# Decode block on one core: wq and wo in one load each, x in four one-row loads, the last PSUM copy on ScalarE

## Chip, core and metric

The kernel runs on one core of a Trainium2 chip. The metric is the device time of one execution in microseconds (us). A core has TensorE (PE, matmul; PEld is its weight load), VectorE (DVE), ScalarE (ACT), GpSimd (POOL) and the sync engine SP, which here issues nearly all loads. Sixteen DMA engines move the data from HBM into the on-chip memory SBUF. Matmuls write PSUM.

## What is computed

One token (x: 1024 numbers, bf16) passes an attention block with a cache and then a gated feed-forward block, each behind a layernorm and with a residual.

```python
q = layernorm(x) @ wq                       # wq 1024 x 4096: 32 heads of 128
k, v = repeat(k_cache, 8), repeat(v_cache, 8)   # 4 kv heads x 65536 positions x 128
p = softmax(q k^T * 128**-0.5)
h = x + (p v) @ wo                          # wo 4096 x 1024
out = h + (gelu(ln(h) @ w_gate) * (ln(h) @ w_up)) @ w_down   # 1024 x 3584 twice, 3584 x 1024
```

The two caches are 64 MB each, wq and wo 8 MB each, the three feed-forward weights 7 MB each: 173.02 MB are read once (counted in millions of bytes), and there is little arithmetic on each byte.

## The kernel before

**The ring.** All large operands go through one SBUF tile, `ring`, of five slots of 16384 bf16 a partition (`CW`, `NBUF`, lines 47 and 48). `load()` (lines 160 to 168) takes the next slots in turn by the counter `at[0]` and issues one load on SP's queue. SP works its issues off in order, and each one waits until the last reader of its slots is done. A K load (`kv_load`, lines 269 to 272) takes one slot, 32 KB to each of 128 partitions; a V load takes two slots, 64 KB to each.

**Start.** ScalarE issues x as one load of four rows of 256 (line 172), which land on partitions 0, 32, 64 and 96 of `x_row`. wq comes in two loads of 4 MB into slots 0 and 1 (lines 174 to 177); the first load is moved to the very front of SP's program (`first_load_leads`, lines 109 to 122). VectorE turns x into columns (line 219) and `layernorm_cols` (lines 197 to 216) makes `xn_bf`, which `padded` spreads out into `xnz`. Eight steps of eight matmuls (lines 246 and 247) make q in `q_ps`, four for each wq load. Copies to SBUF (`evac`, lines 235 to 239: even ones on VectorE, odd ones on ScalarE), transposes and casts then give `wsel` (line 262), the stationary operand of all K scores.

**Attention.** The hand-written list `todo` (lines 378 to 382) sets the order of the 24 K and V loads, and of the work on them. For a K tile VectorE turns four pieces in place (line 281), TensorE makes 32 score matmuls into `qk_ps` (lines 289 to 292), and ScalarE and VectorE copy the scores and take the maximum (lines 301 and 302). For half a V load (one slot) TensorE runs 32 matmuls (lines 340 to 344). The last three V loads are (2, 2), (3, 0) and (3, 2): kv head 2's second half, then kv head 3's two halves. By the counter they lie in slots 3 and 4, in 0 and 1, and in 2 and 3. `v_evac` and `v_end` close a head.

**After attention.** wo comes in two loads of 4 MB (lines 456 and 457), by the counter into slots 4 and 0. w_gate is one load of two slots (line 513; slots 1 and 2), w_up two loads of one slot (line 518; slots 3 and 4), and w_down five loads of falling size laid out one behind the other from slot 0 (lines 538 to 557, `at[0] = 0`). `row_mm` (lines 445 to 449) makes wo's 64 matmuls, c = 0 to 15 from the first load. The residual x is added on TensorE into `f_ps`, the second layernorm gives `hnz`, and gate and up follow. The down matmuls add into `f_ps` as well; `keep_busy` puts matmuls without a use between them. VectorE copies `f_ps` to `o_fin` (line 558), and SP stores it.

Of the kernel before, what the change touches and what calls it, by code (L numbers as in the profile page):

```python
# [17 lines left out]
def kernel(  # L18
# [13 lines left out]
    nc = tc.nc  # L32
    P = 128
    D = A_x.shape[-1]
    Hkv, Sk, Dh = A_k_cache.shape[1], A_k_cache.shape[2], A_k_cache.shape[3]
    HD = A_wq.shape[1]
    Hq = HD // Dh
    rep = Hq // Hkv
    F = B_w_gate.shape[1]
    DC = D // P  # L40
# [6 lines left out]
    CW = 16384  # L47
# [19 lines left out]
    x_row = lead.tile([P, D // 4], BF16, name="x_row")  # L67
# [12 lines left out]
    o_fin = const.tile([P, D // 4], BF16, name="o_fin")  # L80
# [61 lines left out]
    def mm(out, lhsT, rhs, start, stop, loaded=False, tile_position=None, skip_group_check=False):  # L142
        t = nc.tensor
        if not loaded:
            return pe(t.matmul(out, lhsT=lhsT, rhs=rhs, start=start, stop=stop, tile_position=tile_position,  # L145
                               skip_group_check=skip_group_check))
        op = t.add_instruction(mybir.InstMatmult(  # L147
            name=nc.get_next_instruction_name(), engine=t.engine, start_tensor_calc=start, stop_tensor_calc=stop,
            tile_size=(lhsT.shape[0], lhsT.shape[1]), tile_position=tile_position or (0, 0), ldweights=False,
            bass_skip_group_check=skip_group_check,  # L150
            ins=[t.lower_ap(rhs), t.lower_ap(lhsT, for_matmul_weights=True)], outs=[t.lower_ap(out, opt=True)]))
        reuses.add(op.ins.name)
        return pe(op)
# [4 lines left out]
    at = [0]  # L158

    def load(src, off=0):  # L160
        n, w = src.shape[1], src.shape[2]
        units = -(-(off + n * w) // CW)
        o = at[0] * CW + off
        assert o + n * w <= NBUF * CW
        at[0] = (at[0] + units) % NBUF
        tv = ring[:, o:o + n * w]
        nc.sync.dma_start(out=tv.rearrange("p (n w) -> p n w", w=w), in_=src)
        return tv.rearrange("p (n w) -> p n w", w=w)

    wq_v = A_wq.rearrange("(p c) n -> p c n", c=DC)  # L170
    nc.vector.memset(x_row[:], 0.0)
    nc.scalar.dma_start(out=x_row[0:97:32, :], in_=A_x[0, 0].rearrange("(g n) -> g n", g=4))
    assert DC * HD == 2 * CW and DC % 2 == 0
    wq_tiles = []
    for c0 in range(0, DC, DC // 2):
        wq_t = load(wq_v[:, c0:c0 + DC // 2, :])
        wq_tiles.extend(wq_t[:, i, :] for i in range(DC // 2))

    make_identity(nc, ident_bf[:])
    make_identity(nc, ident_f[:])  # L180
# [11 lines left out]
    for bp in range(4):  # L192
        s0 = 64 * (bp // 2) + bp % 2
        nc.vector.tensor_copy(out=esel[:, bp, :, :],
                              in_=ident_bf[:, s0:s0 + 63:2].unsqueeze(1).to_broadcast([P, 4, 32]))
# [27 lines left out]
    def padded(pool, vec, ncols, name, tag=None):  # L223
        t = pool.tile([P, ncols, 32], BF16, name=name, tag=tag or name)
        nc.gpsimd.memset(t[:], 0.0)
        nc.vector.tensor_copy(out=t[:, :, 0], in_=vec)
        return t
# [214 lines left out]
    def row_bank(name):  # L442
        return ps_w.tile([P, 512], F32, name=name, tag="w")

    def row_mm(banks, stat, w2, c, first, last):
        g = c % 4
        for s in range(DS):
            mm(banks[s][32 * g:32 * g + 32, :], stat, w2[:, s * 512:(s + 1) * 512], first, last,
               loaded=(s > 0), tile_position=(0, 32 * g))

    o2z = padded(rows, o2_ps[:], Hq, "o2z")
    wo_v = A_wo.rearrange("(p c) n -> p c n", p=P)
    WN = CW // D
    assert Hq % WN == 0
    at_ps = [row_bank("at_ps") for _ in range(DS)]
    for wc in range(Hq // WN):
        wv = load(wo_v[:, wc * WN:(wc + 1) * WN, :])
        for cc in range(WN):
            c = wc * WN + cc
            row_mm(at_ps, o2z[:, c, :], wv[:, cc, :], c, c < 4, c + 4 >= Hq)  # L460
    at_r = rows.tile([P, DS, 512], F32, name="at_r")
    for s in range(DS):
        evac(at_r[:, s, :], at_ps[s][:], s)
# [1 line left out]
    f_ps = ps_f.tile([P, OW], F32, name="f_ps")  # L465

    def out_mm(stat, mov, first, last, groups=range(4)):
        for g in groups:
            mm(f_ps[32 * g:32 * g + 32, :], stat, mov(g), first, last, tile_position=(0, 32 * g),
               skip_group_check=True)  # L470
# [72 lines left out]
    def keep_busy(n, src):  # L543
        for _ in range(n):
            mm(w_ps[:], ident_bf[:], src, True, True)
# [2 lines left out]
    busy = [3, 2, 1, 0, 0]  # L548
    c0 = 0
    for sz, nb in zip(sizes, busy):  # L550
        at[0] = 0
        wv = load(wd_v[:, c0:c0 + sz, :], c0 * D)
        for cc in range(sz):
            c = c0 + cc
            out_mm(actz[:, c, :], lambda g: wv[:, cc, g * OW:(g + 1) * OW], False, c + 1 == FC)
        c0 += sz
        keep_busy(nb, wv[:, 0, 0:512])
    nc.vector.tensor_copy(out=o_fin[0:97, :], in_=f_ps[0:97, :])
    nc.sync.dma_start(out=out[0, 0].rearrange("(g n) -> g n", n=OW), in_=o_fin[0:97:32, :])


# [28 lines left out]
```

## Time and profile before

| what | value |
|---|---|
| device time, median of 3 runs | 408.42 us (408.33 to 408.43) |
| span of the profiled execution, first to last instruction | 406.9 us |
| median less that span | 1.5 us |
| instructions | 2667 |
| busy: PE, DVE, ACT, POOL | 72%, 50%, 11%, 2% of the span |
| read from HBM | 173.02 MB, 425 GB/s over the span |
| mean granted TensorE clock | 0.912 |

The profile lists no device time of the profiled execution apart from its span, so sums on the profile are set beside the median with the 1.5 us that lie around the span. Times within the profile count from the first instruction. A line of the timeline gives start, duration, engine, source line, operation, what is written from what, and in brackets how long the engine had been idle and what ended that. "SPq" is SP's queue, with the issues of the loads. Matmuls stand under the lines of a helper (145 and 147), and are told apart by their tiles. The trace also records each DMA packet (one row of a load to one partition is one packet) and each of the 16 completion signals of a load, one from each DMA engine; where a text quotes such a record, it says so.

### The profile page before, as it was taken

How to read it: one execution, taken by the hardware profiler on the slowest of the kernel's cores; microseconds unless marked ns; L12 is line 12 of the kernel's file. 1: busy time of each engine (PE TensorE's matmuls, PEld its weight loads, DVE VectorE, ACT ScalarE, POOL GpSimd, SP SyncE). 2: the span in 40 equal slices, each digit the busy share in tenths (PEclk: the TensorE clock that was granted, in tenths of full speed). 3: DMA queues.
4: the chain of work that ended last, by engine and by line, in shares of the span. 5: the costliest groups of instructions: out<-in, count | busy, mean ns of one | idle time of the engine just before them, and what ended most of it. 6: DMA issues, size and time to landing. Idle time of an engine off the chain costs nothing.

```text
span 406.9 us, 2667 instructions
## 1 busy us (share of the span) xinstructions
PE 293.1 (72%) x1495; PEld 60.8 (15%) x743; DVE 202.7 (50%) x185; ACT 44.7 (11%) x67; POOL 7.4 (2%) x17
## 2 busy tenths in 40 slices
PE   1346777769977699597776979976597969636283
PEld 0011111111111112111110111111111101212031
DVE  1118899955978359147971880879433000220110
ACT  1010000022000040100000420000041000100000
POOL 2000000000000000000000000000100000100000
PEclk9986899987989999899996998999989899886889
DMA  9999999999999999999999999999999999999995
GB/s 367 457 412 448 427 419 461 413 444 424 415 464 419 409 499 414 393 438 425 490 414 403 448 425 435 417 457 432 445 438 432 433 399 435 445 436 414 437 419 222
DMA packets 5213, 173.19 MB, mean 426 GB/s; under 512 B 585, under 2 KB 593, under 8 KB 849
## 3 DMA queue, kind: packets, MB, share of 16 engines
q1 hardware_dynamic: 5192, 173.02, 98.7%
q8 instruction: 9, 0.15, 0.1%
q14 instruction: 4, 0.02, 0.0%
q10 hardware_dynamic: 8, 0.00, 0.0%
HBM read 173.02 MB, written 0.00 MB: 425 GB/s over the span
## 4 chain that ended last, share of the span: by engine, by line
DMA 53%; PE 31%; DVE 12%; ACT 2%; issue 0%; SPq 0%; ACTq 0%
DMA ring<-in_A_v_cache_dram 31%; PE acc_ps L147 11%; DVE ring L281 9%; PE qk_ps L145 7%; DMA ring<-in_A_k_cache_dram 7%; DMA ring<-in_B_w_down_dram 7%; DMA ring<-in_B_w_gate_dram 7%; PE qk_ps L147 7%; PE acc_ps L145 4%; DVE mx L302 2%; ACT sc L301 2%; PE wg_ps L145 0%; PE wg_ps L147 0%; DVE pT L330 0%; ACT pe_r L327 0%
## 5 line engine op out<-in xcount | busy, mean ns | idle before, releaser
L281 DVE STREAM_TRANSPOSE ring<-ring 128x2048 uint32<-128x2048 uint32 x64 | 142.7, 2280 | 33.6 <-DMA ring<-in_A_k_cache_dram 33.5
L145 PE MATMUL qk_ps<-ring,wsel 128*128 128x512 bf16 x256 | 100.8, 394 | 35.8 <-DVE mx L302 23.6
L147 PE MATMUL acc_ps<-ring,pT 128*128 128x512 bf16 x384 | 114.1, 409 | 0.0
L147 PE MATMUL qk_ps<-ring,wsel 128*128 128x512 bf16 x256 | 100.6, 393 | 0.0
L145 PE MATMUL acc_ps<-ring,pT 128*128 128x512 bf16 x128 | 52.7, 412 | 20.4 <-DMA ring<-in_A_v_cache_dram 17.6
L145 PEld LDWEIGHTS <-wsel 128*128 128x128 bf16 x256 | 25.4, 99 | 135.1 <-issue 134.4
L301 ACT COPY sc<-qk_ps 128x1024 f32<-128x1024 f32 x16 | 16.2, 1011 | 176.8 <-PE qk_ps L147 176.7
L302 DVE TENSOR_REDUCE mx<-qk_ps 128x1 f32<-128x1024 f32 x16 | 19.6, 1222 | 26.0 <-ACT sc L301 26.0
L145 PEld LDWEIGHTS <-pT 128*128 128x128 bf16 x128 | 13.3, 104 | 119.1 <-issue 113.2
L357 DVE COPY acc_sb<-acc_ps 32x512 f32<-32x512 f32 x8 | 5.4, 672 | 36.6 <-PE acc_ps L147 36.6
L327 ACT ACTIVATE pe_r<-sc,nbias 128x1024 bf16<-128x1024 f32 x16 | 18.2, 1140 | 39.2 <-DVE nbias L322 38.5
L330 DVE STREAM_TRANSPOSE pT<-pe_r 128x1024 bf16<-128x1024 bf16 x16 | 19.0, 1226 | 6.2 <-ACT pe_r L327 6.2
L359 ACT COPY acc_sb<-acc_ps 32x512 f32<-32x512 f32 x8 | 4.6, 577 | 65.0 <-DVE acc_sb L357 65.0
L145 PE MATMUL q_ps<-ring,xnz 128*32 128x512 bf16 x32 | 5.2, 623 | 7.9 <-DMA ring<-in_A_wq_dram 7.9
L145 PE MATMUL wu_ps<-ring,hnz 128*32 128x512 bf16 x32 | 4.7, 503 | 7.8 <-DMA ring<-in_B_w_up_dram 7.8
L145 PE MATMUL wg_ps<-ring,hnz 128*32 128x512 bf16 x32 | 4.6, 517 | 7.7 <-DMA ring<-in_B_w_gate_dram 7.7
L145 PE MATMUL ln_tot<-ln_s,ones_f 128*128 128x1 f32 x8 | 1.9, 312 | 10.8 <-DVE ln_s L199 9.0
L315 DVE TENSOR_REDUCE gm<-mxT_ps 1x8 f32<-1x128 f32 x4 | 1.1, 279 | 16.1 <-PE mxT_ps L156 16.1
L145 PE MATMUL o_ps<-sel,acc_sb 128*128 128x8 f32 x32 | 4.2, 257 | 6.5 <-DVE rl L371 5.7
L145 PE MATMUL f_ps<-ring,actz 128*32 128x256 bf16 x112 | 4.0, 274 | 4.8 <-DMA ring<-in_B_w_down_dram 4.8
L237 DVE COPY q_ev<-q_ps 128x512 f32<-128x512 f32 x1 | 0.7, 692 | 13.3 <-PE q_ps L147 13.3
L237 DVE COPY wg_ev<-wg_ps 128x512 f32<-128x512 f32 x1 | 0.7, 691 | 11.6 <-PE wg_ps L145 11.6
(103 smaller groups left out, 89.2 us busy)
## 6 DMA issues: line engine op xcount, KB each, us to landing
ring<-in_A_k_cache_dram SPq DMA_DIRECT2D x16, 4096.0 KB, 33.9
ring<-in_A_wq_dram SPq DMA_DIRECT2D x2, 4096.0 KB, 16.5
ring<-in_A_wo_dram SPq DMA_DIRECT2D x2, 4096.0 KB, 30.8
ring<-in_B_w_gate_dram SPq DMA_DIRECT2D x1, 7168.0 KB
ring<-in_B_w_up_dram SPq DMA_DIRECT2D x2, 3584.0 KB, 30.5
ring<-in_B_w_down_dram SPq DMA_DIRECT2D x1, 3584.0 KB, 37.1
ring<-in_B_w_down_dram SPq DMA_DIRECT2D x1, 1792.0 KB
ring<-in_B_w_down_dram SPq DMA_DIRECT2D x1, 1024.0 KB, 29.3
```

Of the source, the lines that this page charges most:

```text
L145: return pe(t.matmul(out, lhsT=lhsT, rhs=rhs, start=start, stop=stop, tile_position=tile_position, skip_group_check=skip_group_check))
L147: op = t.add_instruction(mybir.InstMatmult(name=nc.get_next_instruction_name(), engine=t.engine, start_tensor_calc=start, stop_tensor_calc ...
L237: nc.vector.tensor_copy(out=dst, in_=src)
L281: dv(nc.vector.transpose(out=kt[:, c * w:(c + 1) * w], in_=kt[:, c * w:(c + 1) * w]))
L301: ac(nc.scalar.copy(out=sc[:], in_=flat))
L302: dv(nc.vector.tensor_reduce(out=state[("mx", g)][:, li:li + 1], in_=flat, axis=AX.X, op=ALU.max))
L315: dv(nc.vector.tensor_reduce(out=gm[:], in_=mxT_ps[:].rearrange("o (x h) -> o h x", h=rep), axis=AX.X, op=ALU.max))
L327: ac(nc.scalar.activation(out=pe_r[:], in_=state.pop(("sc", g, li))[:], func=ACT.Exp, bias=nbias[:, 0:1], scale=scale, accum_out=lpart[:, ...
L330: dv(nc.vector.transpose(out=pT[:].rearrange("p m c -> p (m c)"), in_=pe_r[:]))
L357: dv(nc.vector.tensor_copy(out=acc_sb[sl, :], in_=acc[sl, c, :]))
L359: ac(nc.scalar.copy(out=acc_sb[sl, :], in_=acc[sl, c, :]))
```

## The change

- wq: one load of 8 MB into slots 0 and 1, 64 KB a partition, where there were two of 4 MB.
- wo: one load of 8 MB, with the counter set to slot 0, so into slots 0 and 1. With the counter going on from there, gate lies in slots 2 and 3 and up in 4 and 0; down starts at slot 1.
- x: four loads of one row each, issued by ScalarE, where there was one of four rows.
- the last copy, `f_ps` to `o_fin`, is ScalarE's.

```diff
-    nc.scalar.dma_start(out=x_row[0:97:32, :], in_=A_x[0, 0].rearrange("(g n) -> g n", g=4))
+    x_v = A_x[0, 0].rearrange("(g n) -> g n", g=4)
+    for g in range(4):
+        nc.scalar.dma_start(out=x_row[32 * g:32 * g + 1, :], in_=x_v[g:g + 1, :])
     assert DC * HD == 2 * CW and DC % 2 == 0
-    wq_tiles = []
-    for c0 in range(0, DC, DC // 2):
-        wq_t = load(wq_v[:, c0:c0 + DC // 2, :])
-        wq_tiles.extend(wq_t[:, i, :] for i in range(DC // 2))
+    wq_t = load(wq_v[:])
+    wq_tiles = [wq_t[:, i, :] for i in range(DC)]
...
-    WN = CW // D
-    assert Hq % WN == 0
+    assert Hq * D == 2 * CW
     at_ps = [row_bank("at_ps") for _ in range(DS)]
-    for wc in range(Hq // WN):
-        wv = load(wo_v[:, wc * WN:(wc + 1) * WN, :])
-        for cc in range(WN):
-            c = wc * WN + cc
-            row_mm(at_ps, o2z[:, c, :], wv[:, cc, :], c, c < 4, c + 4 >= Hq)
+    at[0] = 0
+    wv = load(wo_v[:])
+    for c in range(Hq):
+        row_mm(at_ps, o2z[:, c, :], wv[:, c, :], c, c < 4, c + 4 >= Hq)
...
     for sz, nb in zip(sizes, busy):
-        at[0] = 0
+        at[0] = 1
         wv = load(wd_v[:, c0:c0 + sz, :], c0 * D)
...
-    nc.vector.tensor_copy(out=o_fin[0:97, :], in_=f_ps[0:97, :])
+    nc.scalar.copy(out=o_fin[0:97, :], in_=f_ps[0:97, :])
```

## The prediction

> **What bounds the kernel now.** I read the page's head and queue rows first, then the stretches, then SP's queue in the timeline.
>
> ```profile
> span 406.9 us, 2667 instructions
> ...
> DMA  9999999999999999999999999999999999999995
> ...
> q1 hardware_dynamic: 5192, 173.02, 98.7%
> q8 instruction: 9, 0.15, 0.1%
> ```
>
> The sixteen DMA engines are busy from the first slice to the last but one; SP's loads (q1) fill 98.7% of the span. The stretches (span, busy PE, PEld, DVE, ACT, POOL, clock, DMA share, GB/s) say it by stage:
>
> ```profile
> 31.50:137.00 105.50, 82.22 (x323) 15.33 (x148) 84.79 (x47) 11.96 (x16) 0.00 (x0) 0.89 1.01 433
> 310.00:352.50 42.50, 33.56 (x157) 6.01 (x57) 4.76 (x14) 2.31 (x4) 1.37 (x3) 0.96 1.00 430
> ```
>
> The rate is the same where VectorE is busiest and where it idles, so the stream of loads is the bound and compute fits beside it. The chain of waits runs through compute only because SP's issues wait for free slots, and those come long before the engines run dry. What counts is when the DMA engine that is last delivers the last piece, and the tail behind it:
>
> ```profile
> 403.51 0.29 PE L145 MATMUL f_ps<-ring,actz 128*32 128x256 bf16 x4 [0.21 <-DMA ring<-in_B_w_down_dram]
> 403.85 0.42 DVE L558 CAST o_fin<-f_ps 97x256 bf16<-97x256 f32 x1 [11.71 <-PE f_ps L145]
> 404.30 0.66 SPq L559 DMA_DIRECT2D out_dram<-o_fin  x1
> ```
>
> By the completion records the sixteen engines sign the last down load off between 401.55 and 403.46: they do not wait for each other, and the last one sets the end. The spread is born one engine at a time: it is 0.47 us at 21 us, and after the instruction fetch (q8, 16 KB on one engine) at 45.5 us one engine is 1.4 us behind the rest. Further fetches at 101, 155, 208, 257 and 317 put others back by as much, and the records at 357 and 390 strike engines that had been early; the lag of the last stays near 1.95.
>
> **Fewer, longer rows.** By the packet records a 32 KB row takes 1.213 us in the median and a 64 KB row 2.418. An engine carries 16 rows of 32 KB for wq now, 8 of 64 KB then: 19.41 against 19.34, so -0.07 us, and the same for wo: **-0.14**. The V loads already move 64 KB packets (1024 of them), so they are not split. Two loads fewer give nothing else: the two wq halves land at 12.09 and 21.75, 9.7 us apart, as K tiles do (31.45 and 41.15), so no pause stands between queued loads.
>
> The Trainium skill's "DMA: Bandwidth & Descriptors", section "Anatomy of one DMA", gives every DMA (of GpSimd's kind) a fixed 2 us for setup and completion; taken as it stands, two loads fewer would be 4 us, an estimate of 404.6. The 9.7 us spacing above speaks against it for loads that queue behind each other.
>
> **The start.** q can begin only when all of wq is there.
>
> ```profile
> 7.14 0.63 DVE L219 STREAM_TRANSPOSE x_t<-x_row 128x256 bf16<-128x256 bf16 x1 [5.94 <-DMA x_row<-in_A_x_dram]
> 12.13 0.62 PE L145 MATMUL q_ps<-ring,xnz 128*32 128x512 bf16 x4 [1.82 <-DMA ring<-in_A_wq_dram]
> 21.79 0.62 PE L145 MATMUL q_ps<-ring,xnz 128*32 128x512 bf16 x4 [6.06 <-DMA ring<-in_A_wq_dram]
> 31.47 8.89 DVE L281 STREAM_TRANSPOSE ring<-ring 128x2048 uint32<-128x2048 uint32 x4 [3.62 <-DMA ring<-in_A_k_cache_dram]
> 33.88 0.58 PE L145 MATMUL qk_ps<-ring,wsel 128*128 128x512 bf16 x1 [5.73 <-DVE ring L281]
> ```
>
> The second 32 matmuls run from 21.79 to 25.16, 3.4 us; all 64 behind one wait take at most 6.8, to 28.6. VectorE's last cast for q ended 2.70 after the matmuls (27.86), so 31.3, still ahead of K's first turn at 31.47. `wsel` was ready 4.09 after (29.25), so 32.7, ahead of 33.88. The fourth K load waits for slot 0 until 28.6 instead of 15.8, and the engines have work until 50.4. Cost 0; were that cover gone, up to 3.4 us of delay would enter the K stage, and that has cover of its own: the tightest early issue is the second V load's at 107.73, with the load before it landing from 118.47.
>
> x costs three more issues on ScalarE, 1.08 us each: its table load at 2.19 moves to about 5.4, and ScalarE is next wanted at 25.98. No trace row shows a one-row load. Now each x row is one data packet (5.36 to 5.47) and its signal (6.59 to 6.70), one 32 KB row apart. At best four rows on four engines land as now, at about 7 to 10. At worst all eight small packets alternate on one engine with rows of 2.42 us: 5 + 7 x 2.42 = 22 us. I take the nearer to the worst, 22, since nothing shows that one row is spread. Then `xnz` is ready 4.9 later (7.04 to 11.95 now), at 27; q ends at 34, VectorE is free at 36.5, and K starts 5 us late. The second V load is then issued at 113, still 5 us early. Cost 0 at both ends.
>
> The skill's same page, "Rules for kernel authors", says to coalesce many small transfers, under 64 KB being mostly overhead: this speaks against the four loads. By its 2 us each, an estimate, x would come 6 us later, which the 9.8 us between 11.95 and 21.75 hide; no run here shows one-row loads.
>
> **wo in slots 0 and 1** is where the change can cost.
>
> ```profile
> 303.82 0.33 SPq L167 DMA_DIRECT2D ring<-in_A_v_cache_dram  x1
> 310.73 12.74 SPq L167 DMA_DIRECT2D ring<-in_A_wo_dram  x2
> 340.34 0.33 SPq L167 DMA_DIRECT2D ring<-in_B_w_gate_dram  x1
> 347.25 9.18 SPq L167 DMA_DIRECT2D ring<-in_B_w_up_dram  x2
> ```
>
> Now the halves of wo are issued at 310.73 (slot 4 free) and 323.14 (slot 0 free: V load (3, 0)'s first half is used up), 8 to 20 us ahead of need. The one load needs slot 1 too, so V (3, 0)'s second half used up:
>
> ```profile
> 329.21 0.81 PE L147 MATMUL acc_ps<-ring,pT 128*128 128x512 bf16 x3
> 333.25 0.38 PE L145 MATMUL acc_ps<-ring,pT 128*128 128x512 bf16 x1 [3.23 <-DMA ring<-in_A_v_cache_dram]
> ```
>
> That group is the last: issue at about 330.05. By the packet records V (3, 2), the only load left in the queue, ends on the engines between 330.92 and 332.83. At the start of the kernel, the one place where an issue meets idle engines, the first packets began 1.01 to 1.91 us after it and took up to 0.75 longer than usual, so they flowed as from 1.75 to 2.0. So wo flows from 331.1 to 332.05. Engines that were early stand still for up to 1.1 us; the last one (332.83) does not. Lower bound 0: the early ones stay ahead of the last. Upper bound +1.1: an engine that lost its lead is then put back by the fetches of 357 or 390. The ones struck there are near lag 0.46, ending at 331.4, so they lose up to 0.6 and end that much behind today's last. I take **+0.4**.
>
> Behind wo in SP's queue stand gate, up and down. Gate now waits for slots 2 and 3, so 347.25 in place of 340.34; its first packet was at 350.28, which leaves 1.0 to 2.0 us. Without that cover it costs one for one. The first up load follows at once (slot 4, long free), the second waits as before for wo's first 32 matmuls (356.10), the first down load for the last (357.83); gate and up feed the engines to 386, so 0. wo's matmuls began at 352.51 on `o2z` and wo landed at 352.53: waiting for the whole load shifts them by some tenths, inside the 6.2 us for which gate's matmuls wait for their load (363.2 to 369.5).
>
> **The last copy.** VectorE's 97x256 takes 0.42. ScalarE's rows:
>
> ```profile
> L301 ACT COPY sc<-qk_ps 128x1024 f32<-128x1024 f32 x16 | 16.2, 1011 | 176.8 <-PE qk_ps L147 176.7
> L359 ACT COPY acc_sb<-acc_ps 32x512 f32<-32x512 f32 x8 | 4.6, 577 | 65.0 <-DVE acc_sb L357 65.0
> ```
>
> A line through both gives 0.36 for 256 columns; bounds 0.29 (half of 577) and 0.58. No table load follows the Tanh before line 239's copies, so none is added: **-0.06** (-0.13 to +0.16).
>
> Sum: -0.14 + 0.4 - 0.06 = +0.2 on a span of 406.9. With the 1.5 us around it that is the median, 408.42: forecast **408.6**, own range 407.9 to 409.2.
>
> **Rivals.** *The hole in the stream reaches the last engine* (slower). It decides from an issue of wo at about 330.9, 0.8 later than my sum: V (3, 0) began at 314.4 with slow matmuls (0.63 against 0.38) for some 3.4 us, which costs it 1.7; a second such window, or a longer close of the head before, moves the issue to 331.8 and the flow to 333.6 on all engines. That is +0.8 at the last one, and +2.2 if a later fetch strikes on top: 409.0 to 410.6, say **409.8**. For it: the cover is thin and the clock is granted in such windows. Against: the window is already in this trace once.
> *x lands past 28 us* (slower): K would start over 9 us late and the second V load miss its time. With two long rows between small packets x lands near 30: about +2, **410.4**. Against: the one-row spacing seen now.
> *The engines' lags fall otherwise* (faster): the program's length changes and with it which engine each fetch strikes. The mean signature of the last load is 0.8 ahead of the last one: 408.6 - 0.4 - 0.8 = **407.4**. Against: each fetch seems to strike a new engine, and the loads that change are few.
>
> **Chances.** Forecast 0.60, hole 0.20, x 0.08, lags 0.12. A difference under 0.2% (0.8 us) is about what a measurement of this kernel can tell from no change. So faster 0.12, same 0.60, slower 0.28. Range 407.8 to 410.4: it leaves out the lags (0.12) and the upper part of the two slow cases.
>
> **What would show it.** SP's wo issue at 330 and gate's at 347.3; the DMA slice near 331 down by less than a tenth; x's turn (L219) near 22 and K's turn within 6 us of 31.5; down's last landing near 403.7; ScalarE's copy at 0.36. The prediction is wrong if wo's issue comes at 331 or later, if `xnz` is ready after 33, or if 64 KB rows of wq and wo take other than 2.42 us.

## The result, and the profile after

The changed kernel takes 410.18 us (median of 6 runs, 409.18 to 411.57) against 408.43 (6 runs, 408.33 to 408.63). The ratio is 1.0045, with a 95% interval of 1.0033 to 1.0058: 1.75 us slower. The time lies inside the stated range (407.8 to 410.4), but not where the forecast had it (408.6, no change). What came is what the first rival named, priced at 409.8: a hole in the stream of loads (a time in which DMA engines have no work queued, or only just) that reaches the last engine.

The profiled execution took 410.38 us, with a span of 408.4. The page's head and queue rows:

```profile
span 408.4 us, 2667 instructions
...
DMA  9999999999999899999999999999999999999994
...
q1 hardware_dynamic: 4904, 173.02, 98.5%
q8 instruction: 9, 0.15, 0.1%
```

The same bytes in fewer packets (4904 for 5192), and the DMA engines are still all but full. A loss of 1.5 us in the span is too small to be seen in tenths. It is seen in SP's queue and beside it, in the matmuls on V load (3, 0) and (3, 2) (timeline):

```profile
303.42 0.33 SPq L167 DMA_DIRECT2D ring<-in_A_v_cache_dram  x1
329.64 0.33 SPq L167 DMA_DIRECT2D ring<-in_A_wo_dram  x1
348.10 0.33 SPq L167 DMA_DIRECT2D ring<-in_B_w_gate_dram  x1
348.47 9.08 SPq L167 DMA_DIRECT2D ring<-in_B_w_up_dram  x2
...
328.80 0.81 PE L147 MATMUL acc_ps<-ring,pT 128*128 128x512 bf16 x3
...
332.69 0.59 PE L145 MATMUL acc_ps<-ring,pT 128*128 128x512 bf16 x1 [3.08 <-DMA ring<-in_A_v_cache_dram]
```

wo is issued when the last matmuls on V (3, 0), from 328.80, are done. Between 303.42 and 329.64 nothing is issued, so V load (3, 2) is alone in the queue when wo joins it. By the packet records the first engine is done with that load at 330.50, 0.86 us after wo's issue, and the last at 332.35. The sixteen engines start wo's first row between 330.61 and 333.10. Ten of those first rows take 0.3 to 1.0 us longer than the usual 2.42, and the sum of idle and extra time around this place is 9.3 us over sixteen engines: some 2 us in which engines stand idle, and 7.3 us of longer rows. The same sum for before is 0. At gate, issued 2.5 us before the first engine is done with wo, another 3.3 us are lost, all of it in longer rows. By the completion records wo's last completion signal comes at 353.56 instead of 352.53 and that of the last down load at 405.06 instead of 403.46. The tail behind it:

```profile
405.10 0.29 PE L145 MATMUL f_ps<-ring,actz 128*32 128x256 bf16 x4 [0.23 <-DMA ring<-in_B_w_down_dram]
405.44 0.37 ACT L556 CAST o_fin<-f_ps 97x256 bf16<-97x256 f32 x1 [13.54 <-PE f_ps L145]
405.84 0.65 SPq L557 DMA_DIRECT2D out_dram<-o_fin  x1
```

So the 1.6 us are there before the tail begins, and the tail itself is 0.06 shorter (405.06 to 405.84, against 403.46 to 404.30). The start of the kernel, in the timeline:

```profile
21.96 0.62 DVE L219 STREAM_TRANSPOSE x_t<-x_row 128x256 bf16<-128x256 bf16 x1 [20.75 <-DMA x_row<-in_A_x_dram]
26.77 0.62 PE L145 MATMUL q_ps<-ring,xnz 128*32 128x512 bf16 x4 [1.64 <-DVE xnz L226]
35.44 11.07 DVE L281 STREAM_TRANSPOSE ring<-ring 128x2048 uint32<-128x2048 uint32 x5
37.84 0.38 PE L145 MATMUL qk_ps<-ring,wsel 128*128 128x512 bf16 x1 [2.00 <-ACT wsel L262]
```

x is turned 15 us later than before and K's work starts 4 us later. Whether that costs anything the page can't say; the runs below do.

### The profile page after: what moved, and what is told of

It reads as the page before. It is cut to its first block, busy times and chain, and to the rows that moved or that the text cites. A ratio compares the mean times of both kernels' runs of the same rounds, so it can differ in the third digit from the quotient of the medians.

```text
span 408.4 us, 2667 instructions
## 1 busy us (share of the span) xinstructions
PE 295.0 (72%) x1495; PEld 62.3 (15%) x743; DVE 201.9 (49%) x184; ACT 45.1 (11%) x68; POOL 7.4 (2%) x17
## 3 DMA queue, kind: packets, MB, share of 16 engines
q1 hardware_dynamic: 4904, 173.02, 98.5%
## 4 chain that ended last, share of the span: by engine, by line
DMA 48%; PE 35%; DVE 12%; ACT 3%; issue 1%; ACTq 0%; SPq 0%; DVEq 0%
DMA ring<-in_A_v_cache_dram 30%; PE acc_ps L147 13%; DVE ring L281 8%; DMA ring<-in_B_w_down_dram 7%; PE qk_ps L145 7%; PE qk_ps L147 7%; DMA ring<-in_B_w_gate_dram 6%; DMA x_row<-in_A_x_dram 5%; PE acc_ps L145 5%; DVE mx L302 2%; ACT sc L301 2%; PE q_ps L145 1%; PE q_ps L147 1%; PE wg_ps L145 0%; PE wg_ps L147 0%
## 5 line engine op out<-in xcount | busy, mean ns | idle before, releaser
L145 PEld LDWEIGHTS <-hnz 128*32 128x32 bf16 x64 | 3.4, 122 | 19.9 <-issue 17.6
```

## Experiments

Theory H: the time is lost where a load is issued so late that the DMA engines have nothing else queued. "First dry" below is the moment at which the first of the sixteen engines has finished all loads queued before the load in question. Rivals: X, x comes late; S, the slots (gate's issue moves to 347); R, 64 KB rows are slower. All times are medians, beside runs of the kernel before on the same chip (408.49 for e1 to e4, 408.53 for e5 to e8, 408.61 for e9 to e11).

### e1: the wo edit alone

```diff
-    for wc in range(Hq // WN):
-        wv = load(wo_v[:, wc * WN:(wc + 1) * WN, :])
...
+    at[0] = 0
+    wv = load(wo_v[:])
...
-        at[0] = 0
+        at[0] = 1
         wv = load(wd_v[:, c0:c0 + sz, :], c0 * D)
```

> Before, with the wo edit alone (one load into slots 0 and 1, gate in 2 and 3, down from slot 1). Theory H (the hole: wo is issued with only V (3, 2) left in the queue, about 1 us before the first DMA engine runs dry, and cold first packets follow): the whole loss sits here, 409.6 to 410.4 us, wo's issue at 329.6 to 330.1. Rival X (x is late): 408.4. Rival S (slots: gate's issue moves from 340 to 347): as H, about 410. Rival R (64 KB rows and engines in step are slower): about half the loss, 409.2.

410.02 us, ratio 1.0035 (1.0021 to 1.0049). The loss sits in this edit. wo's issue came at 327.96, earlier than the 329.6 to 330.1 expected: the matmuls on the second half of V (3, 0) took 0.38 us each from the first on, where before and the changed kernel have a stretch of some 3 us with 0.63 each. The profiled execution (410.11) shows more than one hole:

```profile
327.96 0.33 SPq L167 DMA_DIRECT2D ring<-in_A_wo_dram  x1
348.26 0.33 SPq L167 DMA_DIRECT2D ring<-in_B_w_gate_dram  x1
```

Here wo came 2.6 us before the first engine ran dry and little was lost (0.6 us over the sixteen). Gate came 1.6 us before (first engine done with wo at 349.90), and 2.9 us were lost there.

### e2: everything but wo

The changed kernel, with the wo lines of before.

> The changed kernel with wo as before (two loads in slots 4 and 0). Theory H: 408.2 to 408.4, no loss left, though x still lands near 22 us and K starts 4 us late. Rival X: 410, the loss stays. Rival S: 408.3. Rival R: 409.2.

408.24 us, ratio 0.9991 (0.9982 to 1.0000). SP's queue and the end:

```profile
303.09 0.33 SPq L167 DMA_DIRECT2D ring<-in_A_v_cache_dram  x1
310.00 12.74 SPq L167 DMA_DIRECT2D ring<-in_A_wo_dram  x2
339.87 0.33 SPq L167 DMA_DIRECT2D ring<-in_B_w_gate_dram  x1
...
403.43 0.37 ACT L558 CAST o_fin<-f_ps 97x256 bf16<-97x256 f32 x1 [13.35 <-PE f_ps L145]
```

wo is back at 310 and 322, and the copy stands 2 us earlier than in the changed kernel. X falls: x lands as late here (it is turned at 21.95), with no loss. R falls for wq's rows.

### e3: wo in two loads, in the slots of the change

```diff
+    at[0] = 0
     for wc in range(Hq // WN):
...
-        at[0] = 0
+        at[0] = 1
         wv = load(wd_v[:, c0:c0 + sz, :], c0 * D)
```

> Before, with wo in two loads of 4 MB as before but in slots 0 and 1, with gate in 2 and 3 and down from slot 1: the slots of the change, with the first half issued at about 323 (slot 0 free) and the second at 330. Theory H: the queue is never down to one load, so 408.4 (within 0.2). Rival S, the late gate issue at 347: about 410. Rival R: 408.4.

408.83 us, ratio 1.0009 (1.0000 to 1.0017), with runs from 408.33 to 409.89: 0.2 above what H had expected (408.4 within 0.2), and far from S (410).

```profile
322.88 7.24 SPq L167 DMA_DIRECT2D ring<-in_A_wo_dram  x2
347.08 0.33 SPq L167 DMA_DIRECT2D ring<-in_B_w_gate_dram  x1
```

The second half of wo is issued as late as the one load was (329.78), but the first half is queued behind V (3, 2), so nothing is lost there. Gate stands at 347.08, 3.1 us before the first engine is done with wo (350.17), and in this execution (408.69) nothing is lost there either. S as a matter of slots falls. The small loss of the median, and the longer runs, would fit a gate that is now and then later; that was argued and not measured, since only one execution is profiled.

### e4: something queued between V (3, 2) and wo

The changed kernel, with the first up load ahead of wo:

```diff
...
+    wu0 = load(uv[:, 0:GB, :])
     at[0] = 0
     wv = load(wo_v[:])
...
-        wu = load(uv[:, c0:c0 + GB, :])
+        at[0] = 0
+        wu = load(uv[:, c0:c0 + GB, :]) if c0 else wu0
```

> The changed kernel with the first w_up load (slot 4, free since 311) issued ahead of wo; wo stays one load in slots 0 and 1, issued near 330, but 3.5 MB now lie queued between V (3, 2) and wo. wo lands near 361 and gate's matmuls start some 2 us later, inside their slack. Theory H: 408.0 to 408.4, loss gone. Rival X: 410. Rival S: 410, since gate's issue stays at 347. Rival R: 409.5 or more.

408.40 us, ratio 0.9998 (0.9989 to 1.0007).

```profile
311.50 0.33 SPq L167 DMA_DIRECT2D ring<-in_B_w_up_dram  x1
332.14 0.33 SPq L167 DMA_DIRECT2D ring<-in_A_wo_dram  x1
346.83 0.33 SPq L167 DMA_DIRECT2D ring<-in_B_w_gate_dram  x1
```

wo is one load of 64 KB rows, issued later than ever, and x is late; yet the loss is gone, because up is queued from 311.50. This parts H from all three rivals at once. Gate's issue at 346.83 is early here, since wo runs until 358.

### e5: the hole ahead of wo alone

e1, with the first up load issued right behind wo.

```diff
     wv = load(wo_v[:])
...
+    at[0] = 4
+    wu0 = load(uv[:, 0:GB, :])
...
```

> The kernel of e1 (before with the wo edit alone) with the first w_up load (slot 4) issued right behind wo, ahead of gate: wo still meets a queue that holds only V (3, 2), but gate's issue at 347 to 348 now has 3.5 MB queued ahead of it until 359. Theory W (the hole ahead of wo carries the loss of 1.5 us): 409.6 to 410.2. Theory G (the hole ahead of gate carries it): 408.3 to 408.8.

409.68 us (408.20 to 410.96), ratio 1.0026 (1.0013 to 1.0038). That lies where theory W had it (409.6 to 410.2), 1.15 us above before, with an interval of some 0.5 to 1.6 us: the hole ahead of wo carries most of e1's 1.5 us or all of it, and this run can't say whether gate's adds to it. G falls.

```profile
303.04 0.33 SPq L167 DMA_DIRECT2D ring<-in_A_v_cache_dram  x1
329.27 0.33 SPq L167 DMA_DIRECT2D ring<-in_A_wo_dram  x1
329.65 0.43 SPq L167 DMA_DIRECT2D ring<-in_B_w_up_dram  x1
```

wo comes 1.3 us before the first engine is dry (330.55). In this execution (410.35) three engines that were done with V (3, 2) by 330.84 get their first row of wo only at 331.14, 331.70 and 332.10.

### e6 and e7: wq with the copy, and x, each alone

```diff
-    for c0 in range(0, DC, DC // 2):
-        wq_t = load(wq_v[:, c0:c0 + DC // 2, :])
+    wq_t = load(wq_v[:])
...
-    nc.vector.tensor_copy(out=o_fin[0:97, :], in_=f_ps[0:97, :])
+    nc.scalar.copy(out=o_fin[0:97, :], in_=f_ps[0:97, :])
```

> Before, with wq in one load and the last copy on ScalarE. Theory H: 408.3 against 408.4 to 408.5 (64 KB rows -0.07 us, the copy -0.06), q's matmuls 6 to 7 us behind one wait and hidden. Rival R (longer rows cost): 408.6 or more.

408.66 us, ratio 1.0000 (0.9992 to 1.0009): the expected gain of 0.13 is below what this measures. So is the loss with which R would begin (408.6 or more): its median lies there, its ratio of 1.0000 does not, and against R stand e2 and e4, which have the same wq load and lose nothing. q's matmuls ran from 21.74 to 28.2, behind one wait and hidden.

e7 has the change's four loads of x in place of one.

> Before, with x in four one-row loads. wq is still in 32 KB rows, so eight small packets wait behind rows of 1.21 us: x lands near 13 to 14 us instead of 7, all hidden behind wq's second half at 21.8. Theory H: 408.4 to 408.5, no change. Rival X: 409 or more.

408.47 us, ratio 0.9997 (0.9988 to 1.0005): free. The tile's view of e7 gives the landing:

```profile
L174 ACTq DMA_DIRECT2D x_row<-in_A_x_dram x4: 216/287/507, 1.1 to 2.2; - x4
...
L221 DVE STREAM_TRANSPOSE x_t<-x_row x1: 626/626/626, 13.1 to 13.1; 128x256 bf16<-128x256 bf16 x1
```

x is turned at 13.1, as expected from rows of 1.21 us; in the changed kernel, with rows of 2.42, at 21.96.

### e8: e4 with x in one load

> e4 with x in one load: wq and wo in one load each, the first w_up load ahead of wo, the copy on ScalarE. Every part that gains and no hole: 408.1 to 408.3, about 0.2 under before. If x in four loads is free, the same as e4 within 0.1.

408.68 us, ratio 1.0005 (0.9996 to 1.0014), not the 408.1 to 408.3 expected. No version here beats the kernel before by more than its interval. The span of e8 is as short as e4's (406.5 against 406.3), but in ten of its eleven runs 2.0 to 2.2 us lie around it, where the others have 1.8 to 2.0 (2.7 in one run of e9); why stays open.

### e9 and e10: wo sooner, and gate too

The changed kernel with matmuls left out, so that slots come free earlier; the output lacks those positions. e9 leaves out half of those on the second half of V (3, 0); e10 also half of those on the second half of V (3, 2). The edit of e10:

```diff
-        for m0 in range(0, GPL, 4):
+        for m0 in range(16 if g == 3 and li in (1, 3) else 0, GPL, 4):
```

> The changed kernel with half of the matmuls on the second half of V load (3, 0) left out, so the output lacks those positions; nothing else differs, but slot 1 is free 3.5 us earlier and wo is issued near 326.2, over 4 us before the first DMA engine runs dry. Theory H: the hole ahead of wo is gone and the smaller one ahead of gate (issue near 348) stays: 408.4 to 409.0. Rival (rows, slots, x): 410, as the changed kernel.

> As e9, with half of the matmuls on the second half of V load (3, 2) left out too, so gate is issued near 344.5, over 5 us before the engines run dry. Theory H: both holes gone, 408.1 to 408.4, as e2. Rival: 410.

e9: 409.40 us, ratio 1.0021 (1.0012 to 1.0030), more than I expected. e10: 408.30, ratio 0.9993 (0.9984 to 1.0002). SP's queue of e9:

```profile
324.43 0.33 SPq L167 DMA_DIRECT2D ring<-in_A_wo_dram  x1
348.37 0.33 SPq L167 DMA_DIRECT2D ring<-in_B_w_gate_dram  x1
```

and of e10:

```profile
328.63 0.33 SPq L167 DMA_DIRECT2D ring<-in_A_wo_dram  x1
345.54 0.33 SPq L167 DMA_DIRECT2D ring<-in_B_w_gate_dram  x1
```

With wo 6 us ahead of the first dry engine and gate 1.5 us ahead, the median of e9 still loses 0.8 us (0.5 to 1.2), which leaves gate as the place. Its profiled execution lost little (408.78, against 408.61 for before). With both moved forward the loss is gone in the median, while x, wq, wo and the slots are all as in the changed kernel. (The profiled execution of e10 took 409.16, the longest of its eleven: its wo came at 328.63, 1.8 us ahead, and 2.5 us over the sixteen were lost.)

### e11: wo later still

```diff
-    at[0] = 0
+    at[0] = 1
     wv = load(wo_v[:])
...
-        at[0] = 1
+        at[0] = 2
         wv = load(wd_v[:, c0:c0 + sz, :], c0 * D)
```

> The kernel of e1 with wo in slots 1 and 2, gate in 3 and 4, up in 0 and 1 and down from slot 2: wo must wait for the first half of V load (3, 2) as well, so it is issued near 340, 8 to 10 us after the engines ran dry. Theory H: one for one. First rows 1 to 3.5 us after the issue, full flow 0.8 us later, wo's last landing near 363 instead of 352.5: 418 to 420.5 us. Rival (the time is lost elsewhere, and the stream catches up): under 413.

410.92 us (two runs), ratio 1.0057 (1.0038 to 1.0075): far below the 418 to 420.5 of H, and by the number in the rival's range (under 413). But the run did not make the hole that it was to test:

```profile
323.94 0.33 SPq L167 DMA_DIRECT2D ring<-in_B_w_up_dram  x1
339.70 0.33 SPq L167 DMA_DIRECT2D ring<-in_A_wo_dram  x1
```

The first up load lay in slot 0 here, free at 323.9, and stands ahead of wo in SP's queue, which I had not foreseen. So the engines ran dry at 339.07 and not at 330.5, and wo came 0.6 us after that. So it decides nothing between H and the rival, whose forecasts were for a hole of 8 to 10 us; it serves as one more point on the scale below.

**The scale.** From the packet records of the profiled executions: the time from a load's issue until the first engine has nothing else left, and the idle and extra time over sixteen engines.

| hole | issue ahead of the first dry engine, us | lost over 16 engines, us |
|---|---|---|
| e2, gate | 10.0 | 0 |
| e3, gate | 3.1 | 0 |
| e1, wo | 2.6 | 0.6 |
| after, gate | 2.5 | 3.3 |
| e10, wo | 1.8 | 2.5 |
| e1, gate | 1.6 | 2.9 |
| e9, gate | 1.5 | 3.7 |
| e5, wo | 1.3 | 7.2 |
| after, wo | 0.9 | 9.3 |
| e11, wo | -0.6 | 27.1 |

Issued 3.1 us or more ahead, these loads lost nothing; at 2.6 us and less every one lost something, and more with a smaller lead, though not step by step (0.6 at 2.6, 3.3 at 2.5). Each row is one place in one execution. The cause itself is settled by the medians: the wo edit alone brings the loss (e1, against e2), and it goes when another load is queued ahead of wo (e4) or both loads are issued sooner (e10).

**What the scale does not hold.** The lost engine time is only part of the lost kernel time. In the changed kernel 9.3 and 3.3 us over sixteen engines are 0.8 us on each, but its span is 2.1 us longer than that of e2 (408.4 against 406.3), which has the same start. By the completion records the sixteen signals of the last down load come 1.15 us later in the mean than in e2 (403.35 against 402.20), and the last signal 1.71 us after that mean, against 0.84. This lag of the last engine behind the mean is 0.7 to 1.05 us in before, e2, e3, e4, e6, e7 and e8; 1.71 in the changed kernel, 2.13 in e1, 1.86 in e5, 1.49 in e10 and 1.07 in e11; 0.61 in e9. In e1, whose two holes make 0.2 us on each engine, nearly the whole loss is this lag. So a hole seems to cost twice: by the time that engines stand idle or take longer for a row, and by what leaves them further apart, since the last one ends the kernel.

## Why the prediction was right in its range and wrong in its likeliest case

- **The range**: the measured time lies in it because it takes in most of the first rival's 409.0 to 410.6. The forecast's own range (407.9 to 409.2) missed it, and so did the wider one that its three terms give with their bounds (408.15 to 409.54). As a forecast of the likeliest case it failed; that 410.18 is still under 410.4 is partly luck.
- **What bounds the kernel**: right. Moving K's start by 3.4 us cost nothing (e2, 34.88 against 31.47), and where the last down load landed 2.0 us later (405.06 against 403.04 in e2) the span was 2.1 us longer (408.4 against 406.3).
- **64 KB rows**: 2.418 us a row was measured again. The gain of 0.14 us is too small to be told (e6).
- **The start**: x was put at 22 us and turned at 21.96; `xnz` at 27 and q's first matmul came at 26.77; the second V load at 113 and it was issued at 111.27. Free, as said (e7, e2). That x came at 22 is in part luck: the sum was 5 us and seven rows of 2.42, the records show 6.71 and six rows, and the two errors cancel. The cost to ScalarE was put too high: four one-row issues took 1.38 us in all, not 1.08 each.
- The Trainium skill's "DMA: Bandwidth & Descriptors", section "Rules for kernel authors", speaks against many small transfers, and by the fixed 2 us each that the page gives for a DMA of GpSimd's path, an estimate, x would have come 6 us later. Measured, it came 5.9 us later behind rows of 1.21 us (e7, 13.07 against 7.14) and 14.8 behind rows of 2.42: what each small packet waits for is the row ahead of it, so no fixed price fits both.
- **The last copy**: 0.37 against 0.36.
- **wo's hole**: the place was right and the wait was named, but its reach and its price were not. The issue was put at 330.05 and came at 329.64. The failed step is "So wo flows from 331.1 to 332.05" and what follows from it: "Engines that were early stand still for up to 1.1 us; the last one (332.83) does not." It took the start of the kernel, where first packets began 1.01 to 1.91 us after the issue, as a bound. In the changed kernel the last engine was done with V (3, 2) at 332.36, and only two first rows of wo begin after that, at 332.50 and 333.10; they take 3.27 and 3.18 us instead of 2.42. So the last engine did stand idle and did take longer for its row, and wo's last row ended at 353.25, 1.5 us after the 351.7 that eight rows of 2.42 from 332.36 would give. The +0.4 (bound +1.1) became about +1.1 for wo alone by e5's median, with an interval of 0.5 to 1.6.
- **Gate**: the step "which leaves 1.0 to 2.0 us" and its "so 0" rest on an issue at 347.25, 3.0 us before the first engine was done with wo. Such a lead was enough where a run had it (e3, 3.1 us). But gate was issued at 348.10, 2.5 us ahead: the matmuls on V (3, 2) began in a slow stretch (0.59 to 0.63 us each, for some 3 us) that before did not have in that place. And the 1.91 us counted as the longest way from issue to first packet is no safe lead: at 2.5 us first rows were longer by 3.3 us in all, and e9, with 1.5 us, loses 0.8 us in the median.
- The two holes together cost e1 1.5 us. That is less than the sum of 1.1 and 0.8, which the intervals allow; whether the two costs add up was not measured.
- **The rival that came** was given 0.20. It was to decide from an issue of wo at 330.9; it came with an issue at 329.64, 1.3 us sooner, and of the signs that were to show the prediction wrong none was there (wo's issue stayed under 331). Gate's issue (348.10, not 347.3) and down's last landing (405.06, not 403.7) missed what was to be seen.
- **Slips in the working that decided nothing**: from a flow "as from 1.75 to 2.0" after an issue at 330.05 the lower end is 331.8, not 331.1; by the sum used for its lower end the first rival's upper end is 410.4, not 410.6; the second half of wo was issued 17.5 us before the first engine came to it (323.14 and 340.60), so "8 to 20 us ahead of need" should begin at 17.
- **Fetches on top of a hole** were named in the upper bound. In e1's profiled execution the lag of the last engine behind the first grew from 2.07 us at the last up load to 3.42 at the first down load, around the instruction fetch at 390.2; in before it went only from 1.94 to 2.00 around the fetch at 389.9, by the prediction because that fetch struck an engine that was early. In e5, e10 and e11 too the lag grew between two loads with a fetch among them (at 391.3, 359.7 and 367.2); in the executions without a loss, which have such fetches as well, it did not. In the changed kernel it grew at wo itself. This fits, but no run set it apart: what makes the engines end further apart after a hole stays open.
- **The time around the span** was taken as 1.5 us from a span and a median of different executions. In the later runs of before it is 1.8 to 1.9, so its profiled execution took about 408.7.

## What to carry to other kernels

Where the DMA engines are full from end to end, read each load's issue against the moment when the first engine runs out of queued work, and keep 3 us or more between them (3.1 us and more lost nothing here, 2.6 and less did); the matmul or copy that frees the buffer is then part of the critical path, though every engine's own row looks covered. The margin is not the same in every execution: a stretch of slow matmuls (0.63 us for 0.38) of some 3 us in the work that frees the buffer put an issue 1.7 us later (329.64 in the changed kernel, 327.96 in e1). Merging two loads makes the first half wait for the second half's buffer; larger rows gained less here than a measurement can tell. If a merged load must come late, queue another one ahead of it that has a free buffer (e4).

## What was not expected of the hardware

- A load that meets a queue about to run dry reaches its sixteen engines unevenly. In the changed kernel ten of wo's first rows took 2.72 to 3.44 us instead of 2.42, and only six engines had stood idle before theirs; ten others had gone over to wo without a pause. At gate, 2.5 us ahead, no engine stood idle, and first rows were still longer by 3.3 us in all. In e11, where most engines were dry, the first rows began 0.95 to 2.06 us after the issue and most took 2.9 to 3.5 us.
- One-row loads do not share the work: in the changed kernel's packet records the four data packets of x and their four signals go at 6.71, 9.15, 11.57, 14.01, 16.43, 18.86, 21.28 and 21.31, 2.4 us, the time of one row of wq, between each two of the first seven. As one load of four rows they went at 5.36 to 5.47 and 6.59 to 6.70.
- Issuing a four-row load takes ScalarE's queue 1.08 us, a one-row load 0.22 to 0.53.
